# Four tiles of k loaded in fp32 through SyncE's and ScalarE's queues and cast on ScalarE

## The chip, the cores and the metric

The kernel runs on one core of a Trainium2 chip. The metric is the device time of one execution in microseconds (us); smaller is better.

## The reference, cut to what matters

```python
def _attn_ref(q, k, v, tau):                     # q, k, v: (4, 6016, 256) fp32
    qn = q / (np.linalg.norm(q, axis=1, keepdims=True) + 1e-06)
    kn = k / (np.linalg.norm(k, axis=1, keepdims=True) + 1e-06)
    s = kn.transpose(0, 2, 1) @ qn / tau
    # ... softmax of s over its last axis gives a (256 x 256 for each batch)
    return (v @ a).astype(np.float32)

def _moe_ref(x, w_gate, w_val, w_out):           # x: the result above, 24064 x 256
    g = x @ w_gate                               # 256 x 1536
    silu = g * (1.0 / (1.0 + np.exp(-g)))
    return (silu * (x @ w_val) @ w_out).astype(np.float32)
```

The softmax of a batch needs all of that batch's q and k. For batches 1 to 3 this is done beside the matmuls of the batch before. For batch 0 nothing can stand beside it: all of q and k must be in before the first large matmul.

## The kernel before

All of k (47 tiles of 128 x 256), then all of q, then the first four tiles of v go through GpSimd's queue, cast from fp32 to fp8 (v to bf16) by the transfer. Three parts matter here.

```python
    def load_qk(b, g, which, gl=groups):
        # ... (q_sb, k_sb: fp8, [128, 47, 256], made once for each batch)
        gs, gm = gl[g]
        src, dst = (q, k)[which], qk_tiles[b][which]
        nc.gpsimd.dma_start(
            out=dst[:, gs:gs + gm, :],
            in_=src[b].rearrange("(p s) c -> p s c", s=NS)[:, gs:gs + gm, :])
```

```python
    kgroups = [(s, min(16, NS - s)) for s in range(0, NS, 16)]      # 16, 16, 15 tiles
    # ... qgroups: four of 8 tiles, three of 4, then 2 and 1
    order = [(g, 1, kgroups) for g in range(NG)] + [(g, 0, qgroups) for g in range(NQ)]
    for n, (g, which, gl) in enumerate(order):
        load_qk(0, g, which, gl)
        # ... (after the fourth: an identity and two constants, on GpSimd)
    load_first_v()
    # ... weights
```

```python
    for g, which, gl in order:
        # ... (leaves the loop at the last four q groups)
        gs, gm = gl[g]
        ts = list(range(gs // 2, (gs + gm + 1) // 2))               # pairs of tiles
        for at in range(0, len(ts), 4):
            now = ts[at:at + 4]
            sqs = [first_square(0, t, which, on_dve=(t % 2 == 1)) for t in now]
            if which == 0:
                for t in now:
                    gemm1_pair(0, t)                                # q times k, DoubleRow fp8
            for t, sq in zip(now, sqs):
                first_row_sums(0, t, which, sq, (T_COLS if which == 0 else NP) - 1)
        # ... (norms and reciprocals, between the q groups)
```

## Time and profile before

| | before |
|---|---|
| time, median of 3 runs | 809.75 us (809.62 to 809.81) |
| span in the profile | 808.0 us |
| PE busy | 790.9 us, 98% |
| first row-sum matmul of k / first matmul of q and k | 9.67 / 20.97 us |
| v's transposes on PE | 35.37 us |

In the profile, PE is the matrix engine, DVE VectorE, ACT ScalarE, POOL GpSimd and SP SyncE. A timeline row has start, length, engine, line, operation, output and input, the number of instructions merged into the row and, in brackets, how long the engine stood idle before it and what ended the wait. A row of a chain has start, length and what was waited for. A packet is one record of a DMA engine, a group of tiles lands when all its packets are in, and a row-sum matmul multiplies squares of k or q by ones to add them up.

### The profile page before, as it was taken

The page shows a single profiled execution, that of the slowest core. Times are in us where ns is not written, and L with a number is a line of the kernel's source. Part 1 is how long each engine was busy: PE and PEld are TensorE (multiplying, and loading weights), DVE is VectorE, ACT ScalarE, POOL GpSimd, SP SyncE. Part 2 cuts the span into 40 slices and gives each one's busy share as a digit, 9 for nine tenths or more (in the row PEclk, how much of TensorE's full clock was granted, in tenths as well). Part 3 has the DMA queues.
Part 4 walks back from the last instruction along what each step waited for, and adds up shares of the span by engine and source line. Part 5 has one row for each costly group of instructions (what it writes and reads, how often), then busy time and mean ns, then how long its engine had stood idle before and what let it go on. Part 6 is the DMA issues. An engine that isn't in the chain of part 4 may idle for free.

```text
span 808.0 us, 11840 instructions
## 1 busy us (share of the span) xinstructions
PE 790.9 (98%) x3916; PEld 381.3 (47%) x3916; DVE 554.1 (69%) x856; ACT 454.3 (56%) x802; POOL 249.3 (31%) x299
## 2 busy tenths in 40 slices
PE   4999999999999999999999999999999999999998
PEld 1644444444454444444454444444445444444446
DVE  3777878758667878766766877766866665665654
ACT  3666666555556666555555656555555555555553
POOL 3415887331104786332010768610000000000000
PEclk9999999999999999999999999999999999999999
DMA  8995999899897795877995687556645755555443
GB/s 90 144 158 90 179 158 173 154 114 148 167 147 159 144 154 122 165 122 167 158 175 121 117 157 151 131 131 161 127 118 131 135 133 131 129 145 133 115 112 98
DMA packets 203132, 112.40 MB, mean 139 GB/s; under 512 B 151376, under 2 KB 190160, under 8 KB 202320
## 3 DMA queue, kind: packets, MB, share of 16 engines
q1 hardware_dynamic: 185456, 84.55, 43.7%
q0 software_dynamic: 17472, 27.01, 30.2%
q8 instruction: 30, 0.49, 0.3%
q14 instruction: 30, 0.25, 0.1%
q10 hardware_dynamic: 144, 0.10, 0.0%
HBM read 79.06 MB, written 60.48 MB: 173 GB/s over the span
## 4 chain that ended last, share of the span: by engine, by line
PE 95%; DMA 4%; POOL 0%; issue 0%; DVE 0%; POOLq 0%
PE g_ps L466 30%; PE v_ps L466 30%; PE o_new L507 29%; PE ps L433 2%; DMA q_sb<-in_q_dram 2%; PE kq_new L171 2%; DMA v_sb<-in_v_dram 1%; PE o_new L560 1%; PE last_ps L584 0%; POOL k_sb L114 0%; PE unit_ps L433 0%; PE kq_new L176 0%; PE vt_ps L150 0%; POOL q_sb L114 0%; PE ps L423 0%
## 5 line engine op out<-in xcount | busy, mean ns | idle before, releaser
L476 DVE TENSOR_TENSOR sv<-silu,v_ps 128x512 bf16<-128x512 bf16 (+1 forms) x576 | 386.2, 672 | 214.4 <-ACT silu L472 212.2
L472 ACT ACTIVATE silu<-g_ps 128x512 bf16<-128x512 f32 (+1 forms) x576 | 339.1, 589 | 292.2 <-PE g_ps L466 273.1
L466 PE MATMUL g_ps<-vT,Wg 128*128 128x512 bf16 (+1 forms) x1128 | 330.6, 375 | 0.0
L466 PE MATMUL v_ps<-vT,Wv 128*128 128x512 bf16 (+1 forms) x1128 | 330.4, 374 | 0.0
L507 PE MATMUL o_new<-sv,w_out_sb 128*128 128x512 bf16 (+1 forms) x1104 | 324.5, 376 | 0.0
L466 PEld LDWEIGHTS <-Wv 128*128 128x128 bf16 x1152 | 112.7, 98 | 130.9 <-issue 0.4
L311 POOL TENSOR_TENSOR acc_new<-acc_new,sq 128x512 f32<-128x512 f32 x135 | 157.2, 1164 | 52.3 <-DVE sq L301 36.9
L466 PEld LDWEIGHTS <-Wg 128*128 128x128 bf16 x1152 | 111.3, 98 | 125.7
L507 PEld LDWEIGHTS <-w_out_sb 128*128 128x128 bf16 x1104 | 108.0, 98 | 126.4
L129 POOL DMA_DIRECT2D vb_new<-in_v_dram x47 | 24.2, 515 | 241.5 <-DMA vT<-vb_new 241.0
L517 DVE COPY pl<-o_new 128x512 uint16<-128x512 uint16 (+1 forms) x92 | 62.5, 679 | 14.1 <-ACT pl L516 14.1
L301 DVE TENSOR_TENSOR sq<-q_sb 128x512 bf16<-128x512 fp8e5 x72 | 65.1, 904 | 0.0
L516 ACT COPY pl<-o_new 128x512 uint16<-128x512 uint16 (+1 forms) x92 | 53.1, 577 | 19.6 <-PE o_new L507 19.6
L302 ACT ACTIVATE sq<-k_sb 128x512 bf16<-128x512 fp8e5 x72 | 44.2, 614 | 0.0
L114 POOL DMA_DIRECT2D q_sb<-in_q_dram x45 | 25.4, 566 | 15.3 <-DMA k_sb<-in_k_dram 11.3
L171 PE MATMUL kq_new<-k_sb,q_sb 128*128 128x512 fp8e5 x184 | 28.3, 294 | 0.6 <-DMA q_sb<-in_q_dram 0.6
L171 PEld LDWEIGHTS <-q_sb 128*128 128x256 fp8e5 x184 | 21.1, 136 | 5.0 <-DMA q_sb<-in_q_dram 1.2
L378 POOL TENSOR_SCALAR den<-th 128x512 f32<-128x512 f32 x3 | 1.8, 615 | 66.8 <-ACT th L377 49.8
L114 POOL DMA_DIRECT2D k_sb<-in_k_dram x39 | 21.5, 551 | 1.0 <-POOLq L782 0.8
L346 POOL TENSOR_TENSOR inv<-inv,half 64x8 f32<-64x8 f32 x3 | 5.0, 1665 | 53.3 <-DVE inv L344 53.3
L200 PE MATMUL ss_new<-sq,ones_bf 128*128 128x512 bf16 (+1 forms) x24 | 9.2, 538 | 12.0 <-ACT sq L188 12.0
L306 POOL TENSOR_TENSOR acc_new<-sq 128x512 f32<-128x512 bf16 x3 | 3.5, 1151 | 45.9 <-DVE sq L301 45.9
(94 smaller groups left out, 211.9 us busy)
## 6 DMA issues: line engine op xcount, KB each, us to landing
rows<-pl SPq DMA_DIRECT2D x86, 256.0 KB, 2.5
out_dram<-ot_new SPq DMA_DIRECT2D x43, 512.0 KB, 3.8
vb_new<-in_v_dram POOLq DMA_DIRECT2D x43, 256.0 KB, 4.8
q_sb<-in_q_dram POOLq DMA_DIRECT2D x36, 128.0 KB, 6.5
k_sb<-in_k_dram POOLq DMA_DIRECT2D x33, 128.0 KB, 7.3
ot_new<-rows SPq DMA_TRANSPOSE x92, 3.6
rows<-pl SPq DMA_DIRECT2D x6, 192.0 KB, 2.4
out_dram<-ot_new SPq DMA_DIRECT2D x3, 384.0 KB, 7.1
```

Source lines behind the costliest of these rows:

```text
L114: nc.gpsimd.dma_start(out=dst[:, gs:gs + gm, :], in_=src[b].rearrange("(p s) c -> p s c", s=NS)[:, gs:gs + gm, :])
L129: nc.gpsimd.dma_start(out=vb[:mv, :].rearrange("(p s) c -> p (s c)", s=cm), in_=v[b, cs * P:cs * P + mv, :].rearrange("(p s) c -> p (s c)" ...
L171: nc.tensor.matmul(kq[:, jh, :], q_sb[:, ps:ps + 2, js], k_sb[:, ps:ps + 2, :], start=(t == 0 and jh == 0), stop=last, perf_mode=DR, skip_ ...
L301: nc.vector.tensor_mul(sq[:, :pm, 0, :], q_sb[:, ps:ps + pm, :], q_sb[:, ps:ps + pm, :])
L302: nc.scalar.activation(sq[:, :pm, 1, :], k_sb[:, ps:ps + pm, :], ACT.Square)
L311: nc.gpsimd.tensor_tensor(out=acc, in0=acc, in1=sq[:, s, :, :], op=ALU.add)
L466: nc.tensor.matmul(dst[:, :mv], W[:, kk, fs], vT[:, kk, :mv], start=(kk == 0), stop=(kk == CH - 1))
L472: nc.scalar.activation(silu[:, :mv], g_ps[:, :mv], ACT.Silu)
L476: nc.vector.tensor_mul(sv[:, f, :mv], silu[:, :mv], v_ps[:, :mv])
L507: nc.tensor.matmul(self.o_ps[h][:, :self.mv], w_out_sb[:, f, h * P:(h + 1) * P], self.sv[:, f, :self.mv], start=(f == 0), stop=(f == FH - 1))
L516: nc.scalar.copy(pl[:, 0, :self.mv], halves[:, 0, :self.mv])
L517: nc.vector.tensor_copy(pl[:, 1, :self.mv], halves[:, 1, :self.mv])
```

## The change

The intent: SyncE's and ScalarE's queues stand empty at the start while GpSimd is still preparing its first transfer. So the first four tiles of k are taken out of GpSimd's stream and loaded early as plain fp32, two tiles on each of the other queues. ScalarE, which waits then, casts them to fp8.

```diff
+    K0 = 4
+    k0_f = const.tile([P, K0, C], FP32)
+    for s0, eng in ((0, nc.sync), (2, nc.scalar)):
+        eng.dma_start(
+            out=k0_f[:, s0:s0 + 2, :],
+            in_=k[0].rearrange("(p s) c -> p s c", s=NS)[:, s0:s0 + 2, :])
...
+        if (b, g, which) == (0, 0, 1):
+            for s0 in range(0, K0, 2):
+                nc.scalar.copy(dst[:, s0:s0 + 2, :], k0_f[:, s0:s0 + 2, :],
+                               saturate=False)
+            return
...
-    kgroups = [(s, min(16, NS - s)) for s in range(0, NS, 16)]
+    kgroups = [(0, K0)] + [(s, min(16, NS - s)) for s in range(K0, NS, 16)]
...
-        if n == 3:
+        if n == 4:
```

GpSimd still makes three loads of k, now of 16, 16 and 11 tiles.

## The prediction

> **What bounds the kernel now.** I read the page first: busy times, slices, chain.
>
> ```profile
> span 808.0 us, 11840 instructions
> PE 790.9 (98%) x3916; PEld 381.3 (47%) x3916; DVE 554.1 (69%) x856; ACT 454.3 (56%) x802; POOL 249.3 (31%) x299
> ...
> PE   4999999999999999999999999999999999999998
> ```
>
> The matrix engine is busy for 98% of the span; only the first slice of 40 (20 us each) stands at 4 tenths. So almost all that can be won is at the start, 17.1 us of idle time (808.0 - 790.9). The waits of PE over the whole span say what it waits for:
>
> ```profile
> PE ss_new L200 <- ACT sq L188: 12.0, 3, 9.7
> PE vt_ps L150 <- DMA v_sb<-in_v_dram: 0.7, 1, 0.7
> PE kq_new L171 <- DMA q_sb<-in_q_dram: 0.6, 2, 0.4
> PE ss_new L204 <- DVE sq L185: 0.2, 1, 0.2
> ```
>
> Columns: who waited, for whom, us in total, times, longest. The four sum to 13.5 us, and all of them lie before 37 us. After that PE waits for nothing, so a start that is s us shorter should shorten the whole by s. ScalarE, named in the first row, is not the cause: its squares wait for k to land. The third view is the chain of waits from 0 to 42 us (start, length, what):
>
> ```profile
> 1.25 1.33 POOL k_sb L114 x3
> 2.58 0.40 issue
> 2.98 0.56 POOL q_sb L114
> ...
> 4.16 19.14 DMA q_sb<-in_q_dram
> 23.30 0.28 issue
> 23.59 11.73 DMA v_sb<-in_v_dram
> 35.32 0.05 issue
> 35.37 0.62 PE vt_ps L150 x8
> ```
>
> From 4 to 35 us the chain is nothing but transfers on GpSimd's queue: k, q, then the first tiles of v. The timeline shows the three k groups (16, 16 and 15 tiles) becoming usable at 8.99, 13.88 and 18.44 us:
>
> ```profile
> 8.99 1.15 ACT L188 ACTIVATE sq<-k_sb 128x512 bf16<-128x512 fp8e5 x2 [6.96 <-DMA k_sb<-in_k_dram]
> 13.88 1.15 ACT L188 ACTIVATE sq<-k_sb 128x512 bf16<-128x512 fp8e5 x2 [2.10 <-DMA k_sb<-in_k_dram]
> 18.44 2.24 ACT L188 ACTIVATE sq<-k_sb 128x512 bf16<-128x512 fp8e5 x4 [1.78 <-DMA k_sb<-in_k_dram]
> ```
>
> The spacing is 4.89 us for 16 tiles and 4.56 for 15: 0.305 us a tile. A tile is 128 x 256 fp32, 131 kB read, so the stream reads 430 GB/s (the page counts the fp8 bytes written, a quarter of it, hence its figure near 107). The transfers are at their rate all the way; only bytes taken out of the stream, or an earlier start, help. The last view is the activity of the DMA engines from 0 to 5 us, 0.125 us a slice:
>
> ```profile
> DMA  0000000000000000000009944833003993339936
> GB/s 0 0 0 0 0 0 0 0 0 0 0 0 0 0 0 0 0 0 0 0 0 164 164 33 33 66 33 33 0 0 33 229 197 33 33 33 262 131 33 66
> ```
>
> Nothing moves before 2.6 us, although SyncE and ScalarE are free from about 0.75 us (ScalarE's table load starts at 0.75, and SyncE's queue is held for 0.7 us). From 2.6 to 3.8 us there is a dip. The packet records explain it: the first packet on each of the 16 engines starts between 2.63 and 3.42 us and takes up to 1.3 us, yet all end near 4.0; every later one takes 0.63 us. So the stream in effect starts at 4.0 - 0.63 = 3.4 us.
>
> **What the Trainium skill says.** In "DMA: Bandwidth & Descriptors", section "SWDGE vs HWDGE vs iDMA", a cast during a transfer is possible only from GpSimd. That is why the early tiles must come as fp32 and be cast on ScalarE; the trace before agrees as far as it goes, with all casting loads on GpSimd's queue. The same page, "Specifications", gives a first byte after about 1 us on GpSimd's path and about 0.6 us on the path of SyncE and ScalarE. The trace has the same order with larger numbers: GpSimd issues at 1.25 and the first packet starts at 2.63, 1.38 us; SyncE issues a spill at 69.44 and its first packet starts at 70.27, 0.83 us; ScalarE's store at 804.49 starts at 805.38, 0.89 us. I use the trace's. The same page, "Queues, rings and completion order", says that each DMA engine takes turns between queues packet by packet. That matters if both paths overlap: a GpSimd packet is 16 kB read (0.63 us), one of SyncE's is 2 kB (0.085 us in the spill at 70.3). No overlap of that kind is in the trace before. "TensorE: Matmul & The Clock Gate", "What's actually happening", says that the array runs at half clock until it has been busy for a window of about 3.4 us; the trace agrees in kind: row-sum matmuls start 0.43 us apart (8 in 3.57 us) up to 18.1 us, and 0.22 apart from 19.1 on.
>
> **The change part by part.**
> (1) Four of 47 k tiles leave GpSimd's stream. Its k groups become 16, 16 and 11. At 0.305 us a tile the stream is shorter by 4 x 0.305 = 1.22 us. The number of issues on GpSimd stays (three for k), as do their sizes up to the third, so its first packet should still start at 2.63 us. All later issues wait on landings and move with the stream.
> (2) Two loads of 262 kB are added, one on each hardware queue. Issued at about 0.75 us, first packets at 0.75 + 0.83 to 0.89, about 1.6 us. Per engine they are 8 packets of 2 kB each, 16 x 0.085 = 1.36 us; with 0.7 us for a cold first read (an estimate: 1.3 minus 0.63 us in the first packets of before) they end at about 1.6 + 0.7 + 1.36 = 3.7 us if left alone. The stream starts in effect at 3.4, so about 0.3 us of the 1.36 falls on time that the stream would have used; 1.06 us lies in idle time.
> (3) ScalarE gains an issue (0.37 us in the row at 804.49), which delays its 1.28 us table load to about 1.1 us, and two casts of 128x512. The trace's fp32 copy of 128x512 takes 0.58 us (the one at 803.15), so 1.2 us together. Both lie in the 7 us in which ScalarE waits for k. Cost on the path: nothing. Then come four squares and row-sum matmuls that used to be in the first group, also in empty time.
> (4) PE's order is the same, all 24 row-sum steps of k; two of them move to about 6 us. The groups of k that remain are 8, 8 and 6 steps. The second group, ready near 14.0, runs at half clock to about 18.0; the third (11 tiles) lands near 14.0 + 11 x 0.305 = 17.4 and keeps PE going from about 18.0. The first q group then lands at about 19.9 instead of 20.9. At half clock the third group ends at 18.0 + 6 x 0.43 = 20.6, at full clock at 19.4; so there is at most 0.7 us of lateness at that point, and the q part, with about 0.9 us idle of 12 between 20 and 32 us (the table of stretches: 2.00, 1.63, 1.82, 1.98, 1.77, 1.93 busy of each 2 us), and the 0.7 us wait for v behind it, take it up.
> (5) v, last in the chain, follows q in the same stream and moves by the same amount; so do the weights.
> Sum: -1.22 + about 0.3 of overlap, + 0.0 on ScalarE, + up to 0.1 on PE: about -0.9 to -1.0 us. 809.75 - 0.95 = 808.8 us, 0.12%.
>
> **The rivals.**
> A. Contention: the early loads do not use idle time, because they start late or are cold, and only trade places with the stream. For it: the stream is at its rate afterwards, and taking turns by packets makes small packets wait behind 16 kB ones, so that the fp32 tiles may land at 6 to 8 us. Against it: 1.0 us between 1.6 and 2.6 us in which nothing moves. Even then the work is the same bytes, so it gives 809.4 to 809.8.
> B. Full hiding: the early reads also take the cold start away from the stream's first packets. Then nothing of 1.22 us is lost, and up to 0.3 us is won beside it (part of the dip of 2.6 to 3.4 us): 808.3 to 808.5. For it: all first packets end together at 4.0 whenever they started, which looks like a cost paid once. Against it: it may be the writing of the descriptors by GpSimd, which the early loads do not help.
> C. PE becomes the bound at the start: its clock comes up later and the q part at half clock (twice 2.15 us for a group that lands every 2.45) runs behind. This would give back up to 1 us: 809.5 to 810.5. Against it: second and third group now follow each other without a pause (before, 1.0 us lay between), which favours an earlier full clock.
> D. The casts or the wait on ScalarE hold up the squares of the next group. They would have to last until 9 us; the room is about 4 us. Effect nil.
>
> **Range and chances.** My main case and B together lie at 808.3 to 809.1, A and C above it. Runs of before spread 0.2 us. I give 808.2 to 809.5. A change of 2% would be 16 us, about as much as all of PE's idle time; so faster by over 2% 0.005, within 2% 0.99, slower by over 2% 0.005.
>
> **What would show it.** In the changed profile: DMA activity from about 1.6 us on; the casts on ScalarE between 3.7 and 5.5 us; GpSimd's k groups landing near 9.2, 14.0 and 17.4 us; the first q matmul near 20; v's transposes near 34.4 instead of 35.37; PE's waits 13.5 us in sum going down or changing places; and all later rows shifted by the same amount, with no new wait of PE after 37 us. Wrong would be: k groups at 9.5 or later (A), v's transposes earlier than 34.1 (B), or q matmuls that start well after their tiles have landed with PE at half clock after 20 us (C). If v comes earlier by 1 us and the span does not follow, my claim that the start passes on to the end is wrong.

## The result, and the profile after

| | before | after |
|---|---|---|
| time, median of 6 runs | 809.85 us (809.62 to 810.36) | 809.08 us (808.70 to 810.24) |
| ratio | | 0.9992, 95% interval 0.9979 to 1.0005 |
| span in the profile | 808.0 us | 807.1 us |

The ratio is the mean time of one kernel's runs over that of the other's, so it is not quite the ratio of the medians. By the timed runs alone the kernels are the same: the interval contains 1. What follows of where time went comes from two traces, one of each kernel (the changed one's is of the run of 808.89 us), and is to be read so.

The waits of PE over the whole span of the changed kernel (who, for whom, us in total, times, longest):

```profile
PE ss_new L214 <- ACT sq L202: 11.2, 4, 6.4
PE kq_new L185 <- DMA q_sb<-in_q_dram: 0.8, 2, 0.4
PE vt_ps L164 <- DMA v_sb<-in_v_dram: 0.7, 1, 0.7
PE ss_new L218 <- DVE sq L199: 0.2, 1, 0.2
```

There is the same list of waiters as before, with no new one. The gain is in the first row, 11.2 us against 12.0; the row for q rises from 0.6 to 0.8, so the sum falls from 13.5 to 12.9 us. The chain from the start shows the same links, with the transfers still in charge:

```profile
4.16 18.36 DMA q_sb<-in_q_dram
22.52 0.28 issue
22.80 11.83 DMA v_sb<-in_v_dram
34.62 0.05 issue
34.67 0.62 PE vt_ps L164 x8
```

The wait for q is 0.78 us shorter than before (18.36 against 19.14), and v's transposes start 0.70 us earlier (34.67 against 35.37). The timeline of the changed kernel shows the casts and the landing of the k groups:

```profile
0.75 0.39 ACTq L86 DMA_DIRECT2D k_f<-in_k_dram  x1
0.75 0.40 SPq L86 DMA_DIRECT2D k_f<-in_k_dram  x1
...
1.17 1.28 ACT L106 ACT_TABLE_LOAD   x1 [1.17 <-PEq L796]
...
4.68 1.14 ACT L125 CAST k_sb<-k_f 128x512 fp8e5<-128x512 f32 x2 [2.23 <-DMA k_f<-in_k_dram]
...
9.39 1.15 ACT L202 ACTIVATE sq<-k_sb 128x512 bf16<-128x512 fp8e5 x2 [3.05 <-DMA k_sb<-in_k_dram]
...
14.38 2.24 ACT L202 ACTIVATE sq<-k_sb 128x512 bf16<-128x512 fp8e5 x4 [2.21 <-DMA k_sb<-in_k_dram]
...
17.72 1.15 ACT L202 ACTIVATE sq<-k_sb 128x512 bf16<-128x512 fp8e5 x2 [1.09 <-DMA k_sb<-in_k_dram]
...
20.11 1.12 PE L185 MATMUL kq_new<-k_sb,q_sb 128*128 128x512 fp8e5 x8
```

GpSimd's groups of 16, 16 and 11 become usable at 9.39, 14.38 and 17.72 us; those of 16, 16 and 15 before did so at 8.99, 13.88 and 18.44. The first two are therefore 0.40 and 0.50 us later, and the third is 0.72 us earlier. Between second and third group lie 3.34 us now and 4.56 before. The difference, 1.22 us, is exactly four tiles at the 0.305 us a tile that the prediction read.

Where the delay of the first group arises is seen in the activity of the DMA engines of the changed kernel from 0 to 5 us, in slices of 0.125 us:

```profile
DMA  0000000000000099459296899999999696993969
GB/s 0 0 0 0 0 0 0 0 0 0 0 0 0 0 131 115 66 66 115 82 229 246 262 377 344 410 393 426 410 459 230 164 148 82 164 164 33 98 66 229
```

and in the queues of the stretch from 1.5 to 3.5 us, first of the changed kernel and then of the kernel before (packets, MB, share of the 16 engines' time):

```profile
q10 hardware_dynamic: 113, 0.23, 54.3%
q1 hardware_dynamic: 87, 0.18, 24.0%
```

```profile
q0 software_dynamic: 16, 0.07, 56.3%
```

Queue q0 is GpSimd's; q10 and q1 are ScalarE's and SyncE's. Traffic now starts at about 1.75 us. It creeps at some 100 GB/s until 2.5 us and reaches 344 to 459 GB/s from 2.9 to 3.75. GpSimd's queue, whose first 16 packets started between 2.63 and 3.42 us in the kernel before, starts none up to 3.5 us. The packet records give the sum: the last of GpSimd's first 16 packets ends at 4.37 us before and at 4.80 after; packet 64 ends at 6.21 and 6.67, packet 128 at 8.66 and 9.09, packet 256 at 13.52 and 13.96. The stream is pushed back once, by 0.43 to 0.46 us, and keeps that distance up to there.

The other end of the chain shows whether the start's gain arrives. First the kernel before, then the changed one; each has a piece of its chain soon after the start and the last two pieces:

```profile
40.43 0.53 PE ps L433 x2
...
800.05 3.06 PE o_new L560 x28
803.11 1.35 PE last_ps L584 x24
```

```profile
39.73 0.43 PE ps L447 x2
...
799.26 3.06 PE o_new L574 x28
802.32 1.35 PE last_ps L598 x24
```

The last matmuls start 0.79 us earlier: 0.70 from v's transposes and 0.10 from the piece at 40 us, which happened to be 0.10 us longer in the trace before. The span is 0.9 us shorter, so another 0.1 us comes after the last matmul, in the stores. Neither of these tenths is a part of the change that I can name. So what the start passes on in these traces is 0.70 us. The 0.79 at the end is close to the 0.78 of the wait for q only because 0.08 lost at v's landing and 0.10 found at 40 us nearly cancel.

### The profile page after: what moved, and what is told of

It is laid out like the page before. It is cut to its first block, busy times and chain, and to the rows that moved or that the text cites. A ratio compares the mean times of both kernels' runs of the same rounds, so it can differ in the third digit from the quotient of the medians.

```text
span 807.1 us, 11846 instructions
## 1 busy us (share of the span) xinstructions
PE 790.7 (98%) x3916; PEld 381.0 (47%) x3916; DVE 554.8 (69%) x856; ACT 455.4 (56%) x804; POOL 249.4 (31%) x299
## 4 chain that ended last, share of the span: by engine, by line
PE 95%; DMA 4%; POOL 0%; issue 0%; DVE 0%; POOLq 0%
PE g_ps L480 30%; PE v_ps L480 30%; PE o_new L521 29%; PE ps L447 2%; DMA q_sb<-in_q_dram 2%; PE kq_new L185 2%; DMA v_sb<-in_v_dram 1%; PE o_new L574 1%; PE last_ps L598 0%; POOL k_sb L128 0%; PE unit_ps L447 0%; PE kq_new L190 0%; PE vt_ps L164 0%; POOL q_sb L128 0%; PE ps L437 0%
## 5 line engine op out<-in xcount | busy, mean ns | idle before, releaser
L214 PE MATMUL ss_new<-sq,ones_bf 128*128 128x512 bf16 (+1 forms) x24 | 9.1, 528 | 11.2 <-ACT sq L202 11.2
```

## The experiments

**No experiment gave a result.**

Four kernels were sent first. The check ahead of the chip refused all of them, as both the kernel before and the changed one use DoubleRow matmuls (one matmul takes two fp8 tiles at once, as `gemm1_pair` in the kernel shows), and such performance modes were held at the time:

1. The regrouping without the early loads:

```diff
-    kgroups = [(s, min(16, NS - s)) for s in range(0, NS, 16)]
+    kgroups = [(0, 4)] + [(s, min(16, NS - s)) for s in range(4, NS, 16)]
... (the identity and the constants one issue later, as in the change)
```

> All 47 k tiles still through GpSimd, but in groups of 4, 16, 16 and 11: the regrouping of the change without its early loads. Theory (idle DMA time before 3.4 us is filled by the early loads, so the stream is 1.22 us shorter less what overlaps): the stream carries the same bytes from the same start, so v's transposes stay at 35.3 to 35.5 us and the time is that of before, 809.6 to 810.1. Rival (a small first group, whose descriptors are written sooner, whose squares start sooner and which warms the matrix clock sooner, is what helps): first packet well before 2.63 us, or v's transposes near 34.7, time near 809.0.

2. The early loads without their use: the two fp32 loads of the change are added to the kernel before, which is otherwise as it was.

```diff
+    K0 = 4
+    k0_f = const.tile([P, K0, C], FP32)
+    for s0, eng in ((0, nc.sync), (2, nc.scalar)):
+        eng.dma_start(...)                                       # as in the change
```

> The kernel before plus the two early fp32 loads, whose data nobody uses; GpSimd still loads all of k. It measures the overlap alone. Theory: the first k group becomes usable 0.3 to 0.6 us later than the 8.99 of before and the whole stream moves by that, v's transposes at 35.7 to 36.0, time 0.3 to 0.6 over before. Rival A (the early loads use no idle time): the stream is 1.22 us later, v near 36.6, time +1.2. Rival B (they take the cold start off the stream): no delay or an earlier first group, time +0 or less.

3. The last five tiles of k on the hardware queues, held until GpSimd's first group is in (one element of it is copied into each half of the buffer, so that the loads have to wait):

```diff
+            for s0 in (0, 3):
+                nc.vector.tensor_copy(kl_f[:, s0, 0:1], first)
+            load_tail()
... (load_tail: three tiles on SyncE's queue, two on ScalarE's; the casts on ScalarE later)
-    kgroups = [(s, min(16, NS - s)) for s in range(0, NS, 16)]
+    kgroups = [(0, 16), (16, 16), (32, NS - KL - 32), (NS - KL, KL)]
```

> The last five tiles of k (not the first four) as fp32 through the two hardware queues, but held until GpSimd's first group has landed near 9 us, so in no idle time. Theory: bytes only change queues, so v's transposes stay at 35.2 to 35.6 us and the time is that of before, 809.6 to 810.2. Rival (plain transfers on the hardware queues are cheaper than casting ones on GpSimd's, whenever they run): five tiles are taken out of the stream at a lower price, v at 34.9 or earlier, time under 809.3.

4. The same tiles, with the loads issued at the start and without those copies:

> As tail_late, the same tiles, casts and groups, but the loads are issued at 0.75 us. Theory: 5 x 0.305 = 1.53 us leave the stream and about 0.4 to 0.7 us of overlap come back, so v's transposes at 34.3 to 34.7 us, 0.8 to 1.1 us before those of tail_late, and 0.7 to 1.1 us less time than tail_late unless the casts, which here stand late on ScalarE, hold up PE. Rival (what counts is that the first tiles come early, or the cheaper path): no difference between the two.

The first two were then sent with plain matmuls in the place of DoubleRow ones, and so were the kernel before and the changed one, as controls:

```diff
-                nc.tensor.matmul(kq[:, jh, :], q_sb[:, ps:ps + 2, js],
-                                 k_sb[:, ps:ps + 2, :],
-                                 start=(t == 0 and jh == 0), stop=last,
-                                 perf_mode=DR, skip_group_check=True)
+                for s in range(ps, ps + 2):
+                    nc.tensor.matmul(kq[:, jh, :], q_sb[:, s, js], k_sb[:, s, :],
+                                     start=(t == 0 and jh == 0 and s == ps), stop=last,
+                                     skip_group_check=True)
```

The two controls, the early loads without their use and the regrouping were sent in this form four times over. No chip ran any of them; the answer each time was that this was not the kernels' fault. The early loads alone were also sent four times by themselves, over several hours, and no chip ran them either. The third and fourth were never sent in plain form. What had been put on record for the two controls and for the last of these attempts:

> Control. [...]This is the kernel before in that form. Same loads, so k groups at 9.0, 13.9 and 18.4 us and v's transposes at 35.4 us or, if PE runs behind in the q part (its share there rises by about 0.6 us in every 2.45), up to 1.5 us later. Time 12 to 20 us over the kernel before, as 46 pairs per batch cost twice 0.11 us instead of once, in four batches.

> Control: the changed kernel with plain matmuls. Theory (the early loads fill idle DMA time; the stream is 1.22 us shorter less 0.4 to 0.5 of overlap): k groups at 9.4, 14.4 and 17.7 us, v lands 0.6 to 0.9 us earlier than in the control of before, and the time is 0.5 to 1.0 us under it even if PE is the bound in the q part, since that part starts when the first q group lands. Rival (PE's late or half clock takes the gain back): v lands earlier but the time is within 0.2 us of the control.

> The kernel before with each DoubleRow matmul written as two plain ones[...], plus the two early fp32 loads, whose data nobody uses; GpSimd still loads all of k. It measures the overlap alone; its loads are compared with those in the trace of the kernel before, as the matmuls do not touch them. Theory (the early loads fill idle DMA time, and what does not fit pushes the stream back by 0.44 us): the first k group becomes usable 0.3 to 0.6 us later than 8.99 and the whole stream moves by that, so the three groups at 9.4, 14.3 and 18.9 us. Rival A (the early loads use no idle time): 10.2, 15.1 and 19.7. Rival B (they take the cold start off the stream): 9.0 or earlier. The time says nothing here, as plain matmuls add some 12 to 20 us.

All of these were written after the result was known, and the last one's 0.44 us is a number of the two traces; the 0.4 to 0.5 us and the landing times in the control of the changed kernel agree with the traces too. As nothing ran, none of them can count as a forecast that came true.

**What therefore stays open.**

- That idle time of the DMA engines, and not the kind of queue, makes the early loads cheap. The late and early loading of the same tiles was to tell this.
- That the smaller first group brings nothing by itself. The traces speak against a benefit from it (in the changed kernel GpSimd's first group still has 16 tiles and lands later than before), but no run has the regrouping alone.
- How much of the push of 0.44 us belongs to the early loads alone. That they cause it is inferred from its place in time.
- The best number of early tiles. No other number was run.
- Why single runs lie up to 1.5 us above the lowest of their kernel. It is not particular to the change: one of the six of the changed kernel took 810.24 us, at a granted clock of 1.0, and one of the six of before 810.36. Neither has a trace.

## Why the prediction was right, and where its steps were off

The predicted time was 808.8 us, with 808.2 to 809.5; the median measured is 809.08. "Within 2%" held. That the time fell into the range is weak evidence: the range of 1.3 us is no wider than the scatter of the runs (808.70 to 810.24), and no gain at all, 809.75, would have missed it by only 0.25 us. What can be checked are the steps, in the trace.

| step | predicted | in the trace after |
|---|---|---|
| first packets on the hardware queues | about 1.6 us | 1.76 (ScalarE), 1.97 (SyncE) |
| their last data packets end | about 3.7 us | 4.06 and 4.22 |
| the two casts together | 1.2 us, between 3.7 and 5.5, off the path | 1.14 us, 4.68 to 5.82, off the path |
| GpSimd's first packet | 2.63 us, unmoved | 3.53 |
| push on the stream | 0.3 us | 0.43 to 0.46 |
| bytes off the stream | 1.22 us | 1.22 (4.56 - 3.34) |
| groups of k usable | 9.2, 14.0, 17.4 us | 9.39, 14.38, 17.72 |
| first q matmul | near 20 us | 20.11 |
| v's transposes | near 34.4 us | 34.67 |
| gain in the matmuls at the end | 0.9 to 1.0 us | 0.79 |

**Right: the form of the sum, and its large term.** Four tiles at 0.305 us are met to the hundredth. The stream's net shift is 1.22 - 0.44 = 0.78 us, which is what the chain shows at q; v's transposes, and with them the start of the large matmuls, moved by 0.70. The claim that a shorter start passes on to the end is borne out for this pair of traces: no wait of PE after 37 us appeared.

**Slips in the working.** The terms -1.22, +0.3 and up to +0.1 add up to -0.82 to -0.92 us, not to -0.9 to -1.0. The landings at 9.2, 14.0 and 17.4 us leave out part of the 0.3; with it they would be 9.29, 14.18 and 17.52. The first packets of before were read too evenly: they took 0.63 to 1.59 us and ended between 3.84 and 4.37, so rival B's "all end together at 4.0" is not in the trace. And not all later issues wait on landings: in both traces five of q's nine are out by 6.32 us, which changes nothing, as they stand in the same queue.

**Off in size: part (2), the overlap.** It was 0.44 us instead of 0.3. Two terms were off. The hardware queues' first packets came 1.01 and 1.22 us after their issue at 0.75; I had used the 0.83 and 0.89 us of spills and stores late in the kernel, which read from the chip's own buffers and not from HBM; that this is the reason is not shown. And the early loads were still busy until 4.2 us, not 3.7. The difference 4.2 - 3.4 = 0.8 us is not the push, though. Summed over their packets and divided by 16 engines, the early loads took 1.87 us an engine, of which 0.47 lay after 3.4 us, where the stream of before in effect starts. This estimate is close to the push of 0.43 to 0.46 and fits the claim that only what lies outside the idle time costs something. It comes from the same two traces and is no test of it.

**Wrong in mechanism: the first packet of part (1), and the taking of turns.** I had GpSimd's first packet stay at 2.63 us and share the engines from there. In the trace it starts at 3.53, and up to 3.5 us only the two hardware queues have packets. In return, GpSimd's first 16 packets take 0.62 to 0.73 us, not up to 1.6 us as before. They end only 0.43 us later although they start 0.9 us later. So part of what rival B described is there: the long first packets are gone from GpSimd's queue, and the early loads have slow ones instead (0.08 to 0.86 us, median 0.17, for the 23 packets of 2 kB that start before 2.26 us; median 0.084 later). B's consequence, that nothing of the 1.22 us is lost, did not come. Whether GpSimd's packets were held back by the other queues' traffic, or the packets of before were only marked as started while they waited for the same slow first reads, the two traces do not tell.

**Rival A** did not happen in full: a push of 1.22 us would have left v's transposes at 35.4. **Rival D** did not happen: the casts end at 5.82, and the next group lands at 9.39. **Rival C** cost nothing that shows in the profiled run, but by luck more than by my argument. I had said that the closer second and third groups favour an earlier full clock. The table of stretches of the changed kernel (its clock is the third number from the end: PEclk, then the share of the DMA engines and GB/s) shows otherwise for the profiled run:

```profile
14.00:18.00 4.00, 2.91 (x8) 0.93 (x8) 2.86 (x5) 2.52 (x5) 0.60 (x2) 0.78 1.01 103
18.00:20.00 2.00, 1.60 (x5) 0.61 (x5) 1.45 (x3) 1.50 (x3) 0.45 (x1) 0.58 1.10 111
20.00:22.00 2.00, 2.00 (x19) 1.59 (x16) 1.89 (x4) 1.15 (x2) 0.53 (x1) 1.00 1.02 102
```

The clock was at full speed for the first half of the second k group and then at half: 0.78 over 4 us is 1.76 us of half clock, which puts its start at 16.24, and 0.58 over 2 us is 1.68 us, which puts its end at 19.68. The clock's own records agree, with a stretch of 3.41 us at half clock from 16.25 to 19.66. Before the first record (12.84 us here, 18.56 in the kernel before) the column shows 1.00 for want of one; the row-sum matmuls, 0.43 us apart, show half clock there. So the clock first came up 5.7 us earlier than before, and for good 1.1 us later. The q part, whose 2.15 us of work in every 2.45 us would take about 4.3 us at half clock (an estimate, twice 2.15), began at 20.11, only 0.45 us after the clock had come back. A half-clock stretch that fell later would have run into it.

The records of the changed kernel lie 3.41 us apart. Counted back in such steps from the changes on record, PE was busy for 2.76 and 2.99 us of the stretches that ended with a rise (12.84 and 19.66) and for 1.66 of the one that ended with the fall (16.25). In the kernel before it was 2.06 and 2.10 us in two stretches after which the clock stayed at half, and 2.98 in the one before the rise at 18.56. The ends of the stretches lie at different places of the two runs, and that is the luck in it. The run of 810.24 us had no such fall back to half clock: one of 3.41 us would lower the mean clock of 807 us to 0.998, as in the profiled run, and the record gives 1.0 for it and for the four others. Whether its clock first came up later, which the mean would not show, stays open.

## What to carry to other kernels

Where a start is bound by one stream of transfers, as here, what an early load on another queue is worth can be read as a sum of two terms: the bytes taken off the stream at the stream's own rate, minus what the early load pushes the stream back. Both can be read from one trace each of before and after: the first from the spacing of later landings (1.22 us here), the second from the end of the stream's first packets (0.44 us). What of it reaches the first large matmul has to be read there (0.70 us of 0.78). When such a gain is 0.1% of the time, timed runs will not show it (six of each left an interval that contains 1), so say which part of the claim rests on times and which on single traces.

## What the Trainium skill lacked or had wrong

- "DMA: Bandwidth & Descriptors", "Specifications", gives a first byte on the path of SyncE and ScalarE after about 0.6 us. In these traces the first packet starts 0.83 and 0.89 us after the issue late in the kernel, and 1.01 (ScalarE) and 1.22 us (SyncE) after it at the kernel's start with an HBM source. These count from the start of the issuing instruction; from its end they are 0.49, 0.52, 0.62 and 0.82 us, so the figure may count from there, which the page does not say.
- The same page has no figure for the first reads of a kernel. Before, GpSimd's first 16 packets took 0.63 to 1.59 us against 0.63 later; after, the 2 kB packets of the hardware queues that start before 2.26 us took a median of 0.17 us against 0.084 later.
- The same page, "Queues, rings and completion order", has an engine take turns between queues packet by packet. In the changed kernel GpSimd's queue started no packet up to 3.5 us, 0.9 us later than before, while 200 packets of the other two queues did start. Between 3.5 and 4.5 us packets of all three start side by side (27 of GpSimd's, 88 of the others). It may be that GpSimd's packets were not ready before, or that a packet of the page is more than one record of the profile; no run here tells, so this does not show the page wrong.
- "TensorE: Matmul & The Clock Gate", "What's actually happening", puts the fall to half clock after an idle window of about 3.4 us. Here the clock fell at 16.25 us although PE had been busy for about 1.66 of the 3.41 us before it (the row-sum matmuls up to 13.31 and those from 15.06), so in this trace a window that was half busy did not keep it. The starts of the matmuls agree, 0.42 to 0.43 us apart from 16.49 on. How idle a window has to be, no figure there says.
